# Another order of steps and loads at the start of an attention and FFN kernel

## The chip, the cores and the metric

The kernel runs on one core of a Trainium2 chip. The metric is the time on the device, in microseconds (us), of one execution. The core has five engines with a program each, which run side by side and meet at semaphores: TensorE (PE; its weight loads are shown as PEld), VectorE (DVE), ScalarE (ACT), GpSimdE (POOL) and SyncE (SP), which issues the loads.

## The reference

Eight batches of attention with eight heads, 576 tokens and 64 features to a head; keys and values are means over windows of 8 tokens, so there are 72 of each. Its result is the input of a feed-forward network, 4608 tokens x 512, with 2048 hidden units:

```python
k_p = k.reshape(B, H, Sp, pool, D).mean(axis=3)      # pool = 8, Sp = 72
v_p = v.reshape(B, H, Sp, pool, D).mean(axis=3)
scores = scale * np.matmul(q, k_p.transpose(0, 1, 3, 2))
scores = scores - np.max(scores, axis=-1, keepdims=True)
attn = np.exp(scores)
attn = attn / (np.sum(attn, axis=-1, keepdims=True) + 1e-09)
out = np.matmul(attn, v_p)                           # B x H x S x D
x = out.transpose(0, 2, 1, 3).reshape(B * S, H * D)  # 4608 x 512
h = x @ w_in                                         # 512 x 2048
g = h * (1.0 / (1.0 + np.exp(-1.702 * h)))
y = g @ w_out                                        # 2048 x 512
```

All of it is float32.

## The kernel before

**Tiling.** The work runs in eight rounds. Round b computes the attention of batch b for its 576 tokens; the first 512 go to the FFN as chunk b, and the last 64 of every batch are collected and make a ninth chunk. A batch is handled in two pieces (tokens 0 to 255, and 256 to 575) and, in a piece, in four groups of two heads. FFN products split each float32 operand into a high part that TensorE takes at its fast float32 mode and a low remainder, and add three products (high-high, high-low, low-high). Chunks 0 and 1 go through `dense` (L2217), chunk 0 in two halves of 256 tokens; the other seven through `pair` and `outputs` (L2410, L2621), which save products by sums and differences of quarters.

**Names, which the steps of the prediction use.** `kv`, `tl`: a batch's keys and values, and their last 64 rows, as loaded. `red_k`, `red_v`: sums over windows of 8 tokens; in batch 0 DVE makes the first half of the keys' (`red0_k0`, L1427) and PE the other three by adding eight products with the identity (L1420). `tps`: the windows of the last rows, a product with a 0/1 matrix `members`. `kbd`, `vbd`, `tbd`: these sums laid out block by block with a mask (DVE, L1452 and L1565). `kps` then `k`: the keys transposed by products with the identity `ident`, and copied by ACT (L1632). `qps` then `qt`: the same for q (L1699, copy at L1706). `sps`: scores (L1727). Softmax: `nm` maxima (L1750), `sc` difference (L1758) and exponential on ACT (L1779), sums and reciprocal (L1784 to L1794), `main` and `tail` weights for the first 64 keys of each head and for the last 8 (L1799). `apt`, `tpt`: these transposed (L1871), copied to `ah`, `at`; `pav`: weights by values (L1974, L1977); `x`: its result, split into a high part (ACT, L2008) and a remainder (DVE, L2011). `h`: the first FFN product (L2230 to L2232). `raw`, `e`, `w`: a piece of `w_in` or `w_out` as loaded, its rounding by bits (ACT and DVE shifts, L2136 to L2151) and the cast to the two parts (L2163). `warm`: a product of `ident` with itself whose result nobody uses. In names, `qps0_1_2` is batch 0, piece 1, group 2. A float32 product shows as two records in the trace, or in PE's program as two instructions.

**What sets the order.** The body of the kernel emits nothing; it puts tasks in a list, each with an engine, an estimated duration, what it reads and writes, and a due time. `Plan.order` (L998) simulates the engines with these estimates and returns an order. Two tables written into the file then change it: `PLACES` gives a task's name an offset to its rank in that order, and `SWAPPED` names tasks that run on their other engine: a copy on DVE instead of ACT, or a subtraction, difference or shift on DVE instead of POOL. The offsets carry some 3300 names, and the second table some 510. `WARMS` emits warm-up products right ahead of named tasks:

```python
WARMS = {"PE tps0#0": 16, "PE qps0_0#0": 2, "PE h0_0#0": 2}
order = plan.order()
for n, t in enumerate(order):
    t.rank = n + PLACES.get(t.name, 0)
    if t.name in SWAPPED:
        t.swap()
order.sort(key=lambda t: t.rank)
for t in order:
    for _ in range(WARMS.get(t.name, 0)):
        keep_warm()
    t.emit()
```

Each engine runs its own instructions strictly in that order, and SP issues loads in it too; a ring of buffers (four PSUM banks for `o` and two kinds of two) makes a task wait for an earlier user of its place. So an offset in the table sets which instruction an engine will wait at, and what stands behind it.

Of the kernel before, what the change touches and what calls it, by code (L numbers as in the profile page):

```python
# [19 lines left out]
POOL = 8  # L20
# [20 lines left out]
    "ACT ah0_0#0": 9.64, "ACT ah0_0#1": 9.8235, "ACT ah0_0#2": -10.8, "ACT ah0_0#3": -26.5, "ACT ah0_1#0": 14.6667,  # L41
    "ACT ah0_1#1": 25.0, "ACT ah0_1#3": -14.2857, "ACT ah1_0#0": 66.5, "ACT ah1_0#1": 30.0, "ACT ah1_0#2": 9.8333,
    "ACT ah1_0#3": 28.0769, "ACT ah1_1#0": 63.1852, "ACT ah1_1#1": 59.4444, "ACT ah1_1#2": 81.0,
    "ACT ah1_1#3": 73.6, "ACT ah2_0#0": 97.8462, "ACT ah2_0#1": 15.4545, "ACT ah2_0#2": 56.3077,
    "ACT ah2_0#3": -24.7273, "ACT ah2_1#1": -1.6667, "ACT ah2_1#3": 7.6667, "ACT ah3_0#1": -26.7,
    "ACT ah3_0#2": 50.6667, "ACT ah3_0#3": 38.4444, "ACT ah3_1#0": 13.1818, "ACT ah3_1#1": 16.8571,
    "ACT ah3_1#2": 39.3333, "ACT ah3_1#3": 51.0, "ACT ah4_0#1": -3.3333, "ACT ah4_0#3": 26.125, "ACT ah4_1#2": 3.25,
    "ACT ah5_0#0": -28.3333, "ACT ah5_0#1": -4.5, "ACT ah5_0#2": 5.3333, "ACT ah6_0#0": -86.3333,
    "ACT ah6_0#1": -39.5, "ACT ah6_0#2": -53.5909, "ACT ah6_0#3": -59.5, "ACT ah6_1#1": 4.3333,
    "ACT ah6_1#3": 10.25, "ACT ah7_0#0": -19.0, "ACT ah7_0#3": 7.6667, "ACT ah7_1#0": -19.5, "ACT ah7_1#2": 3.5,  # L50
    "ACT at0_0#1": -28.5, "ACT at0_1#0": -4.0, "ACT at0_1#1": -4.0, "ACT at1_0#0": 77.2667, "ACT at1_0#1": 71.4,
    "ACT at1_1#0": 75.6296, "ACT at1_1#1": 67.1111, "ACT at2_0#0": -4.0, "ACT at2_0#1": 31.7143,
    "ACT at2_1#0": 12.4444, "ACT at3_0#0": 26.0, "ACT at3_0#1": 22.5, "ACT at3_1#1": -4.375, "ACT at4_0#0": -10.5,
    "ACT at4_0#1": -10.4286, "ACT at4_1#1": 4.75, "ACT at5_0#0": -6.5, "ACT at5_0#1": -13.5, "ACT at5_1#1": -2.3333,
    "ACT at6_0#0": -47.6667, "ACT at6_0#1": -48.2857, "ACT at6_1#0": -47.2308, "ACT at6_1#1": -38.0,
    "ACT at7_0#0": -38.25, "ACT at7_0#1": -42.125, "ACT at7_1#0": -43.3333, "ACT at7_1#1": -40.6667,
    "ACT cs2_0#0": 4.75, "ACT cs2_0#2": 2.3333, "ACT cs2_0#5": -5.6, "ACT cs2_0#7": -7.1429, "ACT cs2_1#0": 6.2857,
    "ACT cs2_1#2": 13.6, "ACT cs2_1#4": 11.6667, "ACT cs2_1#5": 3.3333, "ACT cs2_2#0": 8.3333, "ACT cs2_2#3": -6.8,
# [4 lines left out]
    "ACT cs3_0#0": -7.3333, "ACT cs3_0#6": -9.5, "ACT cs3_1#0": 23.2, "ACT cs3_1#1": 14.7143,  # L63
    "ACT cs3_1#2": 27.7143, "ACT cs3_1#6": 11.3333, "ACT cs3_1#7": -3.0, "ACT cs3_2#2": -16.25,
    "ACT cs3_2#5": -3.75, "ACT cs3_2#6": 7.75, "ACT cs3_3#1": -12.7143, "ACT cs3_3#2": 18.2857,
    "ACT cs3_3#3": -13.3333, "ACT cs3_4#0": 13.8333, "ACT cs3_4#2": 23.0, "ACT cs3_4#3": 10.5, "ACT cs3_4#5": 11.8,
    "ACT cs3_4#6": -16.25, "ACT cs3_5#0": 7.4, "ACT cs3_5#1": -4.5, "ACT cs3_5#2": -16.0, "ACT cs3_5#3": -12.8182,
    "ACT cs3_5#4": -21.6667, "ACT cs3_5#6": 17.0, "ACT cs3_6#0": -16.3333, "ACT cs3_6#1": -19.5,
    "ACT cs3_6#2": -1.25, "ACT cs3_6#3": -16.8333, "ACT cs3_6#4": -27.6471, "ACT cs3_6#5": -33.0588,
    "ACT cs3_6#6": -20.1765, "ACT cs3_6#7": -49.75, "ACT cs3_7#0": -38.25, "ACT cs3_7#1": -61.25,  # L70
    "ACT cs3_7#2": -22.6, "ACT cs3_7#3": -57.25, "ACT cs3_7#4": -41.7, "ACT cs3_7#5": -20.0, "ACT cs3_7#7": -2.3333,
    "ACT cs4_0#0": -11.0, "ACT cs4_0#1": -9.0, "ACT cs4_0#4": -5.8, "ACT cs4_0#5": -1.1429, "ACT cs4_0#6": 14.4286,
    "ACT cs4_0#7": 17.2857, "ACT cs4_1#1": 4.5, "ACT cs4_1#5": 8.2, "ACT cs4_1#6": 16.5, "ACT cs4_2#2": -29.0,
# [6 lines left out]
    "ACT cs4_7#6": -50.8571, "ACT cs4_7#7": -3.7143, "ACT cs5_0#2": 17.25, "ACT cs5_0#4": -17.125,  # L80
    "ACT cs5_0#7": -8.5, "ACT cs5_1#0": -6.8333, "ACT cs5_1#1": -8.5, "ACT cs5_1#5": 12.6, "ACT cs5_1#6": 23.5,
# [5 lines left out]
    "ACT cs6_0#5": -6.0, "ACT cs6_0#6": 12.0, "ACT cs6_1#1": -9.75, "ACT cs6_1#3": -4.5, "ACT cs6_1#4": -11.0,  # L87
# [6 lines left out]
    "ACT cs7_0#0": -6.8571, "ACT cs7_0#1": -9.7143, "ACT cs7_0#3": -19.2222, "ACT cs7_0#6": 13.7778,  # L94
    "ACT cs7_1#0": -1.6667, "ACT cs7_1#1": -14.6667, "ACT cs7_1#3": -12.0, "ACT cs7_1#4": -12.4286,
    "ACT cs7_1#5": -14.3333, "ACT cs7_1#7": -4.5, "ACT cs7_2#1": -1.5, "ACT cs7_2#2": 6.0, "ACT cs7_2#7": -3.5,
    "ACT cs7_3#1": 3.0, "ACT cs7_3#5": 3.3333, "ACT cs7_4#0": 8.3333, "ACT cs7_4#1": 3.3333, "ACT cs7_4#5": 3.25,
    "ACT cs7_5#5": 3.25, "ACT cs7_6#5": 3.25, "ACT cs8_0#0": -2.3333, "ACT cs8_0#2": -2.0, "ACT cs8_0#7": -7.6667,
    "ACT cs8_1#0": 7.0, "ACT cs8_2#2": 8.6667, "ACT cs8_2#5": 4.5, "ACT cs8_3#1": 3.0, "ACT cs8_3#5": 3.3333,
    "ACT cs8_4#0": 8.3333, "ACT cs8_4#1": 3.3333, "ACT cs8_4#5": 3.6667, "ACT cs8_5#5": -1.7143,  # L100
    "ACT cs8_6#0": -8.2857, "ACT cs8_6#1": -4.6667, "ACT cs8_6#3": -2.6667, "ACT cs8_6#4": -2.6667,
    "ACT cs8_6#5": -1.3333, "ACT cs8_7#0": -5.5, "ACT cs8_7#1": -3.5, "ACT cs8_7#3": -2.6667,
    "ACT cs8_7#4": -2.6667, "ACT e#10": -89.9, "ACT e#12": 9.0, "ACT e#14": 8.6, "ACT e#15": -5.5,
    "ACT e#16": -5.6667, "ACT e#18": 39.6, "ACT e#20": 29.6667, "ACT e#21": -47.8889, "ACT e#22": 42.7143,
    "ACT e#24": 43.4545, "ACT e#25": 40.7143, "ACT e#26": 30.7273, "ACT e#27": -8.8571, "ACT e#28": 174.5,
    "ACT e#29": 161.1667, "ACT e#3": 42.08, "ACT e#30": 93.5455, "ACT e#31": 173.8, "ACT e#32": 141.6,
    "ACT e#4": -84.6667, "ACT e#5": -6.72, "ACT e#6": -37.0, "ACT e#7": -39.4706, "ACT e#8": -75.8333,
    "ACT e#9": -4.0, "ACT g0_0#2": -55.3333, "ACT g0_0#6": 10.0, "ACT g0_256#1": -51.5, "ACT g0_256#2": -88.2,
    "ACT g0_256#3": -134.8571, "ACT g0_256#5": -32.3077, "ACT g0_256#7": -17.2222, "ACT g1_0#0": 20.0,
    "ACT g1_0#1": 23.5714, "ACT g1_0#11": 14.4545, "ACT g1_0#12": -20.3333, "ACT g1_0#13": -17.1429,  # L110
    "ACT g1_0#15": -24.25, "ACT g1_0#2": -6.6667, "ACT g1_0#4": -15.25, "ACT g1_0#5": -15.6667, "ACT g1_0#6": -8.75,
    "ACT g1_0#7": -27.2857, "ACT gh0_0#0": -7.3333, "ACT gh0_0#2": -52.2, "ACT gh0_0#5": 14.6,
    "ACT gh0_0#6": 10.6667, "ACT gh0_0#7": -9.6667, "ACT gh0_256#1": -55.8, "ACT gh0_256#2": -91.1333,
    "ACT gh0_256#3": -146.7143, "ACT gh0_256#5": -36.0769, "ACT gh0_256#7": -21.6667, "ACT gh1_0#0": 17.0,
    "ACT gh1_0#1": 16.4286, "ACT gh1_0#11": 21.2857, "ACT gh1_0#12": -8.3077, "ACT gh1_0#15": -18.0,
    "ACT gh1_0#2": -7.1111, "ACT gh1_0#4": -25.7778, "ACT gh1_0#5": -6.0, "ACT gh1_0#6": -12.375,
    "ACT gh1_0#8": -4.4286, "ACT gh2_0#0": 6.4, "ACT gh2_1#1": 13.6667, "ACT gh2_1#3": 5.3333, "ACT gh2_2#2": 28.0,
    "ACT gh2_3#0": -18.5, "ACT gh2_3#2": -15.3333, "ACT gh2_3#3": -30.3333, "ACT gh2_4#2": 5.5455,
    "ACT gh2_4#3": -7.6364, "ACT gh2_5#0": 8.8571, "ACT gh2_5#1": 43.5, "ACT gh2_5#3": -12.6667,
    "ACT gh2_6#0": 21.0909, "ACT gh2_6#1": -3.8, "ACT gh2_6#3": -8.2857, "ACT gh2_7#0": 14.4, "ACT gh3_0#2": -7.8,  # L120
    "ACT gh3_1#0": 8.3333, "ACT gh3_1#2": 11.4286, "ACT gh3_2#0": -24.6667, "ACT gh3_2#2": 11.5,
    "ACT gh3_4#0": 22.8, "ACT gh3_4#2": -20.0, "ACT gh3_5#0": -10.6667, "ACT gh3_5#2": 14.3333,
    "ACT gh3_6#1": -30.7647, "ACT gh3_6#2": -16.8824, "ACT gh3_6#3": -45.0, "ACT gh3_7#0": -14.8,
    "ACT gh3_7#1": -29.6, "ACT gh3_7#2": -12.0, "ACT gh4_0#1": 7.5714, "ACT gh4_0#2": 22.1429,
    "ACT gh4_1#1": 9.6667, "ACT gh4_2#0": -22.5, "ACT gh4_2#2": -4.2, "ACT gh4_2#3": -16.75, "ACT gh4_3#1": 30.4,
    "ACT gh4_4#0": 36.3, "ACT gh4_4#1": 15.1667, "ACT gh4_4#2": -5.0, "ACT gh4_4#3": -10.4, "ACT gh4_5#0": 38.75,
    "ACT gh4_5#1": 33.5, "ACT gh4_6#0": 21.7273, "ACT gh4_6#2": -22.3636, "ACT gh4_6#3": -34.8182,
# [2574 lines left out]
```

## Time and profile before

| | |
|---|---|
| three executions | 892.00, 891.79, 890.77 us; median 891.79 |
| the profiled execution | 892.42 us, of which the trace spans 890.6 |
| TensorE clock granted | 1.00 |
| PE busy | 879.3 us (99%) |
| DVE, ACT, POOL busy | 630.1 (71%), 543.8 (61%), 314.6 (35%) |
| start of the trace to the first `h` product | 35.52 us |
| moved by DMA in the span | 176.67 MB, mean 198 GB/s |

The profile is one execution. A row of a timeline has its start, the busy time of a run of like instructions, engine and line, the operation, what it writes and reads, the count, and in brackets how long the engine was idle before it and what it waited for. A row of a list of waits has the total, the number and the longest of such idle times. The time that a group is busy is counted to the end of its last instruction; the next one often starts before that. Line numbers are those of the kernel before; after the change those behind the tables are higher by 11.

### The profile page before, as it was taken

To read this page: it belongs to the slowest core of one execution; us is meant where nothing else is said; L and a number is where in the kernel's file an instruction comes from. 1 tells how busy PE (TensorE), PEld (TensorE's weight loads), DVE (VectorE), ACT (ScalarE), POOL (GpSimd) and SP (SyncE) were. 2 spreads that over 40 slices of the span, in tenths; PEclk is the share of its full clock that TensorE was granted. 3 is DMA by queue.
4 is the path that set the end of the run, shared out by engine and by line. 5 is a ranking of instruction groups with operands and counts; after the bars stand their busy time and mean duration, and the time that the engine had idled before them with its cause. 6 is when DMAs were issued, how large, how long until landed. Compare 5 with 4: busy or idle time off the path is not lost.

```text
span 890.6 us, 15774 instructions
## 1 busy us (share of the span) xinstructions
PE 879.3 (99%) x5432; PEld 785.8 (88%) x5432; DVE 630.1 (71%) x1255; ACT 543.8 (61%) x1245; POOL 314.6 (35%) x309
## 2 busy tenths in 40 slices
PE   7999999999999999999999999999999999999997
PEld 6889988888899998898999998989998989998986
DVE  5877889888888886698878887787677843222332
ACT  4986665356676754667576766686568563344433
POOL 2888565664412233221521161236323460000000
PEclk9999999999999999999999999999999999999999
DMA  9964454657467657678775677667664675556541
GB/s 254 370 223 134 124 151 156 234 200 215 156 202 228 223 181 245 182 226 241 219 218 181 176 233 219 220 203 250 175 205 145 201 235 186 172 190 205 166 142 48
DMA packets 145262, 176.67 MB, mean 198 GB/s; under 512 B 85664, under 2 KB 96928, under 8 KB 145184
## 3 DMA queue, kind: packets, MB, share of 16 engines
q1 hardware_dynamic: 140336, 166.89, 60.5%
q10 hardware_dynamic: 4848, 8.78, 2.8%
q8 instruction: 43, 0.70, 0.3%
q14 instruction: 35, 0.29, 0.1%
HBM read 150.47 MB, written 25.17 MB: 197 GB/s over the span
## 4 chain that ended last, share of the span: by engine, by line
PE 94%; SPq 2%; ACT 1%; DMA 1%; issue 0%; DVE 0%; ACTq 0%
PE ha L2435 18%; PE hb L2435 13%; PE o L2639 12%; PE o L2638 12%; PE o L2637 11%; PE sps L1727 4%; PE h L2230 3%; PE h L2232 3%; PE h L2231 3%; PE o L2274 3%; PE o L2272 3%; PE o L2273 3%; DMA raw<-in_moe_w_out_dram 1%; SPq L1317 1%; PE pav L1966 1%; PE pav L1969 1%
## 5 line engine op out<-in xcount | busy, mean ns | idle before, releaser
L2639 PE MATMUL o<-w,glall 128*128 128x512 f32 x448 | 176.3, 394 | 0.0
L2637 PE MATMUL o<-w,ghall 128*128 128x512 f32 x448 | 176.3, 394 | 0.0
L2638 PE MATMUL o<-w,ghall 128*128 128x512 f32 x448 | 176.0, 393 | 0.0
L2489 POOL TENSOR_TENSOR glall<-shared,ghall 128x256 fp32r<-128x256 f32 x88 | 70.4, 805 | 215.8 <-ACT shared L2482 144.3
L2639 PEld LDWEIGHTS o<-w,glall 128*128 128x128 f32 x448 | 84.2, 188 | 18.5
L2435 PEld LDWEIGHTS ha<-xs,ws 128*128 128x128 f32 x672 | 92.6, 189 | 7.6 <-ACT shared L2450 1.0
L2435 PE MATMUL ha<-xs,ws 128*128 128x256 f32 x672 | 99.2, 283 | 0.0
L2474 ACT ACTIVATE ghall<-shared 128x256 fp32r<-128x256 f32 x150 | 61.5, 415 | 60.9 <-DVE shared L2457 32.5
L2435 PE MATMUL hb<-x,ws 128*128 128x256 f32 x672 | 95.5, 284 | 0.0
L2435 PEld LDWEIGHTS hb<-x,ws 128*128 128x128 f32 x672 | 89.1, 189 | 4.5 <-DVE shared L2457 0.5
L2637 PEld LDWEIGHTS o<-w,ghall 128*128 128x128 f32 x448 | 84.6, 189 | 9.1
L2638 PEld LDWEIGHTS o<-w,ghall 128*128 128x128 f32 x448 | 84.1, 188 | 9.1
L2457 DVE TENSOR_TENSOR shared<-shared,hb 128x256 f32<-128x256 f32 x112 | 46.5, 415 | 55.8 <-PE hb L2435 40.9
L2450 ACT COPY shared<-ha 128x256 f32<-128x256 f32 x94 | 34.8, 370 | 65.0 <-PE ha L2435 63.8
L2489 POOL TENSOR_TENSOR glall<-gall,ghall 128x256 fp32r<-128x256 f32 x45 | 33.4, 746 | 103.4 <-ACT gall L2482 67.9
L2230 PE MATMUL h<-x,w 128*128 128x256 f32 (+1 forms) x192 | 63.0, 328 | 0.7 <-ACT g L2247 0.5
L2482 ACT ACTIVATE shared<-shared 128x256 f32<-128x256 f32 x150 | 61.0, 415 | 3.7 <-ACT osb L2190 0.5
L2232 PE MATMUL h<-x,w 128*128 128x256 f32 (+1 forms) x192 | 61.3, 319 | 0.0
L2231 PE MATMUL h<-x,w 128*128 128x256 f32 (+1 forms) x192 | 61.2, 319 | 0.0
L2260 POOL TENSOR_TENSOR gl<-g,gh 128x512 fp32r<-128x512 f32 x30 | 41.0, 1367 | 50.4 <-ACT gh L2252 35.6
L2489 DVE TENSOR_TENSOR glall<-shared,ghall 128x256 fp32r<-128x256 f32 x62 | 29.5, 477 | 35.8 <-ACT shared L2482 27.3
L2435 PEld LDWEIGHTS ha<-x,shared 128*128 128x128 f32 x336 | 46.7, 189 | 4.8 <-ACT shared L2450 0.8
(193 smaller groups left out, 2039.1 us busy)
## 6 DMA issues: line engine op xcount, KB each, us to landing
ws<-wd SPq DMA_DIRECT2D x168, 512.0 KB
shared<-wd SPq DMA_DIRECT2D x56, 256.0 KB
out_dram<-osb ACTq DMA_DIRECT2D x32, 256.0 KB
wd<-stage SPq DMA_DIRECT2D x16, 512.0 KB
raw<-in_moe_w_in_dram SPq DMA_DIRECT2D x15, 512.0 KB
raw<-in_moe_w_out_dram SPq DMA_DIRECT2D x15, 512.0 KB
kv_False<-in_k_dram SPq DMA_DIRECT2D x28, 256.0 KB
kv_True<-in_v_dram SPq DMA_DIRECT2D x28, 256.0 KB
```

Source lines behind the costliest of these rows:

```text
L2230: nc.tensor.matmul(o, lhsT=w[:, 0, j], rhs=xs[:, 0], start=j == 0, stop=False)
L2231: nc.tensor.matmul(o, lhsT=w[:, 1, j], rhs=xs[:, 0], start=False, stop=False)
L2232: nc.tensor.matmul(o, lhsT=w[:, 0, j], rhs=xs[:, 1], start=False, stop=j == NJ - 1)
L2260: engine.tensor_tensor(out=gl(), in0=g(), in1=gh().bitcast(F32), op=ALU.subtract)
L2435: nc.tensor.matmul(o, lhsT=wv()[:, r, jj], rhs=xo(k, jj), start=start and n == 0, stop=n == len(terms) - 1,  skip_group_check=not start,)
L2457: lambda: nc.vector.tensor_tensor(out=part(i), in0=part(i), in1=hb()[:, half * 256 : half * 256 + 256], op=ALU.add),
L2474: lambda: nc.scalar.activation(out=gh(), in_=src(), func=AF.Gelu_apprx_sigmoid),
L2482: lambda: nc.scalar.activation(out=part(i), in_=src(), func=AF.Gelu_apprx_sigmoid),
L2489: engine.tensor_tensor(out=gl(), in0=part(i), in1=gh().bitcast(F32), op=ALU.subtract)
L2637: nc.tensor.matmul(o(), lhsT=gh()[:, tok], rhs=w()[:, 0], start=start, stop=False)
L2638: nc.tensor.matmul(o(), lhsT=gh()[:, tok], rhs=w()[:, 1], start=False, stop=False)
L2639: nc.tensor.matmul(o(), lhsT=gl()[:, tok], rhs=w()[:, 0], start=False, stop=stop)
```

## The change

The change lies in the two tables alone: 1139 of the offsets in `PLACES` differ, and in `SWAPPED` 36 names are gone and 40 are new. No function, no estimate and not `WARMS` is touched, and the arithmetic is as it was. From about the middle of chunk 1 the programs of PE, and further on those of the other engines, are the same again: the last 4305 of PE's 5203 instructions stand in the same order, the last 1015 of DVE's, 1075 of ACT's, 217 of POOL's and 473 of SP's. PE's instructions are the same in number, and so are SP's; DVE has six more.

Two rows or so of the tables, as an example:

```diff
@@ PLACES @@
-    "DMA kv0#3": 8.1, "DMA kv0#4": -5.5, "DMA kv0#5": -4.3333, "DMA kv0#6": -32.3, "DMA kv0#7": -38.4,
+    "DMA kv0#0": 3.3, "DMA kv0#4": 52.75, "DMA kv0#5": 46.625, "DMA kv0#6": 15.2, "DMA kv0#7": 23.8889,
...
+    "PE qps0_0#0": -16.7143, "PE qps0_0#1": -18.5714, "PE qps0_1#0": -37.4, "PE qps0_1#1": -41.25,
...
@@ SWAPPED @@
+    "ACT main7_1#8", "ACT qt0_0#0", "ACT qt0_0#1", "ACT qt0_0#2", "ACT qt0_1#2", "ACT qt0_1#3", "ACT stage#11",
 WARMS = {"PE tps0#0": 16, "PE qps0_0#0": 2, "PE h0_0#0": 2}
```

What that makes of the engines' programs is seen in their first rows. A row is a line of the kernel, the operation, what it writes and reads with buffer numbers, the size, and a count where alike instructions follow each other.

SP, the first loads. Before:

```order
L2105 DMA raw4_131<-in_moe_w_in_dram 128x4x256
L1317 DMA kv0_145<-in_k_dram 128x1x512 x2
L1378 DMA tl0_148<-in_k_dram 64x8x64
L1378 DMA tl0_148<-in_v_dram 64x8x64
L2539 DMA q0_0_151<-in_q_dram 128x8x64 x2
L2105 DMA raw0_154<-in_moe_w_in_dram 128x4x256
L1317 DMA kv0_156<-in_k_dram 128x1x512 x2
```

Now:

```order
L2550 DMA q0_0_131<-in_q_dram 128x8x64 x2
L1389 DMA tl0_147<-in_v_dram 64x8x64
L1389 DMA tl0_147<-in_k_dram 64x8x64
L2116 DMA raw0_174<-in_moe_w_in_dram 128x4x256
L1328 DMA kv0_181<-in_k_dram 128x1x512 x2
L2116 DMA raw4_189<-in_moe_w_in_dram 128x4x256
L1328 DMA kv0_198<-in_k_dram 128x1x512 x2
```

The q tiles come first, and the first keys behind the last rows and a weight piece.

PE, the start of the program. Before:

```order
L2600 MATMUL warm_135<-ident_79 128x128 x17
L1556 MATMUL tps0_188<-tl0_148,members_141 128x512
L2600 MATMUL warm_135<-ident_79 128x128 x2
L1699 MATMUL qps0_0_0_196<-ident_79,q0_0_151 128x128 x2
L1699 MATMUL qps0_0_1_199<-ident_79,q0_0_151 128x128 x2
L1607 MATMUL kps0_0_202<-ident_79,kbd0_190 128x64x2 x2
```

Now:

```order
L2611 MATMUL warm_136<-ident_79 128x128 x2
L1710 MATMUL qps0_0_0_139<-ident_79,q0_0_131 128x128 x2
L1710 MATMUL qps0_0_1_142<-ident_79,q0_0_131 128x128 x2
L2611 MATMUL warm_136<-ident_79 128x128 x16
L1567 MATMUL tps0_170<-tl0_147,members_150 128x512
L1618 MATMUL kps0_0_200<-ident_79,kbd0_193 128x64x2 x2
```

The q transposes have moved ahead of `tps0`; of the warm-up products, which go with their tasks, 16 now stand between the two.

DVE, after its masks are made, up to the first keys. Before:

```order
L1427 TENSOR_REDUCE red0_k0_159<-kv0_145 128x128
L1452 TENSOR_TENSOR kbd0_190<-red0_k0_159,mask2i_84 128x256
L1565 TENSOR_TENSOR tbd0_192<-tps0_188,mask_90 128x512
L2151 TENSOR_SCALAR raw4_131<-e4_133 128x512
L1750 TENSOR_REDUCE nm0_0_220<-sps0_0_0_215 128x2x2
```

Now:

```order
L1576 TENSOR_TENSOR tbd0_172<-tps0_170,mask_90 128x512
L2162 TENSOR_SCALAR raw0_174<-e0_176 128x512
L1717 COPY qt0_0_0_187<-qps0_0_0_139 128x256
L1438 TENSOR_REDUCE red0_k0_191<-kv0_181 128x128
L1463 TENSOR_TENSOR kbd0_193<-red0_k0_191,mask2i_84 128x256
```

The layout of the last rows, a weight piece's shift and a q copy that ACT made before stand ahead of the first key sum.

PE again, from the last scores of piece 0 of batch 0. Before:

```order
L1727 MATMUL sps0_0_3_279<-k20_211,qt0_0_3_270 128x144 x2
L1420 MATMUL red0_v1_287<-kv0_165,ident_79 128x128 x8
L1699 MATMUL qps0_1_0_309<-ident_79,q0_1_168 128x128 x2
L1699 MATMUL qps0_1_0_309<-ident_79,q0_2_170 128x64
L1699 MATMUL qps0_1_1_313<-ident_79,q0_1_168 128x128 x2
L1699 MATMUL qps0_1_1_313<-ident_79,q0_2_170 128x64
L1420 MATMUL red0_v0_326<-kv0_222,ident_79 128x128 x8
L1871 MATMUL apt0_0_3_360<-ident_79,main0_0_353 128x128 x2
L1871 MATMUL apt0_0_2_363<-ident_79,main0_0_353 128x128 x2
L1871 MATMUL tpt0_0_372<-ident_79,tail0_0_358 64x128 x2
```

Now:

```order
L1738 MATMUL sps0_0_2_266<-k20_217,qt0_0_2_256 128x144 x2
L1710 MATMUL qps0_1_1_285<-ident_79,q0_1_245 128x128 x2
L1710 MATMUL qps0_1_1_285<-ident_79,q0_2_283 128x64
L1710 MATMUL qps0_1_0_290<-ident_79,q0_1_245 128x128 x2
L1710 MATMUL qps0_1_0_290<-ident_79,q0_2_283 128x64
L1882 MATMUL tpt0_0_306<-ident_79,tail0_0_304 64x128 x2
L1431 MATMUL red0_v1_316<-kv0_294,ident_79 128x128 x8
L1882 MATMUL apt0_0_3_325<-ident_79,main0_0_310 128x128 x2
L1882 MATMUL apt0_0_0_333<-ident_79,main0_0_310 128x128 x2
```

The transposes of the softmax's tail (`tpt0_0`) now stand ahead of both value sums.

1387 rows, old and new, of tables (PLACES, SWAPPED) are left out of this document.

## The prediction

> **What bounds the kernel now.** I read the table of stretches first, because one share over 890 us says nothing of the stage that the change touches. Its columns are the stretch, its length, the busy time of PE, PEld, DVE, ACT and POOL with instruction counts, the granted clock, the DMA share and GB/s.
>
> ```profile
> 0.00:36.00 36.00, 30.43 (x193) 26.23 (x193) 22.23 (x51) 22.42 (x46) 15.36 (x19) 1.00 0.96 293
> 36.00:260.00 224.00, 223.10 (x1278) 193.73 (x1277) 191.86 (x329) 142.85 (x277) 136.42 (x115) 1.00 0.58 183
> 260.00:850.00 590.00, 589.81 (x3752) 534.57 (x3751) 403.87 (x847) 363.69 (x889) 162.80 (x176) 1.00 0.66 206
> ```
>
> From 36 us on PE is busy without a gap, and PE's instructions are the same in number before and after. So the change can be paid only where PE stands: 5.6 us of the first 36, and the last fraction of a microsecond behind. Next the list of PE's waits, first up to 36 us, then (last two rows) behind it; columns are total, count and longest.
>
> ```profile
> PE sps L1727 <- ACT k L1632: 1.2, 2, 0.7
> PE red_k L1420 <- DMA kv<-in_k_dram: 1.1, 1, 1.1
> PE tps L1556 <- DMA tl<-in_v_dram: 0.9, 1, 0.9
> PE qps L1699 <- DVE sps L1784: 0.5, 1, 0.5
> PE kps L1607 <- DVE kbd L1452: 0.3, 1, 0.3
> PE kps L1613 <- DVE tbd L1565: 0.2, 1, 0.2
> ...
> PE h L2230 <- ACT g L2247: 0.5, 1, 0.5
> ...
> PE h L2230 <- ACT x L2008: 0.2, 1, 0.2
> ```
>
> Third, PE's timeline, for when each step of the first batch runs (start, busy time of the group, what, and idle before it):
>
> ```profile
> 8.65 1.10 PE L1556 MATMUL tps<-tl,members 128*128 128x512 f32 x2 [0.92 <-DMA tl<-in_v_dram]
> ...
> 10.56 0.43 PE L1607 MATMUL kps<-ident,kbd 128*128 128x128 f32 x2
> ...
> 14.83 2.02 PE L1420 MATMUL red_k<-kv,ident 128*128 128x128 f32 x16 [1.08 <-DMA kv<-in_k_dram]
> 16.69 0.38 PE L1699 MATMUL qps<-ident,q 128*128 128x128 f32 x2
> 17.37 0.44 PE L1607 MATMUL kps<-ident,kbd 128*128 128x128 f32 x2 [0.30 <-DVE kbd L1452]
> 17.64 0.53 PE L1613 MATMUL kps<-ident,tbd 128*128 128x32 f32 x4
> 18.83 1.25 PE L1727 MATMUL sps<-k,qt 128*128 128x144 f32 x8 [0.66 <-ACT k L1632]
> 19.99 2.02 PE L1420 MATMUL red_v<-kv,ident 128*128 128x128 f32 x16
> ...
> 25.67 0.63 PE L1871 MATMUL apt<-ident,main 128*128 128x128 f32 x4
> ...
> 32.47 1.99 PE L1727 MATMUL sps<-k,qt 128*128 128x144 f32 x12
> ...
> 35.52 0.36 PE L2230 MATMUL h<-x,w 128*128 128x256 f32 x1
> ```
>
> Nearly everything is a chain here: key sums, keys, scores, softmax, first FFN product `h` at 35.52. Whatever delays `h` is paid in full, since nothing idles behind it that could take it back, beyond the last two waits of the list, .7 us.
>
> **The change, part by part.** *Loads, then the warm-up.* The q tiles are loaded first now, and their four transposes (`qps0_0_0`, `qps0_0_1`) stand on PE ahead of `tps0`. But the 16 warm-up products are tied to `tps0`, so they stand between the two. Before, the same products ran while the loads were awaited. Their price, in two halves of that stretch:
>
> ```profile
> 1.36:6.21 4.85, 4.85 (x22) 4.85 (x23) 1.00 0.89 257
> 6.35:7.57 1.22, 1.22 (x13) 1.20 (x11) 1.00 0.99 200
> ```
>
> So .22 us a record until PE has worked 4.85 us, and .094 after it, though the granted clock reads 1.00 in both. When q lands I take from the first load:
>
> ```profile
> 4.42 0.63 ACT L2136 ACTIVATE e<-raw 128x512 f32<-128x512 f32 x1 [2.40 <-DMA raw<-in_moe_w_in_dram]
> ...
> 8.12 1.91 DVE L1427 TENSOR_REDUCE red_k<-kv 128x128 f32<-128x1024 f32 x1 [4.78 <-DMA kv<-in_k_dram]
> 10.07 0.42 DVE L1452 TENSOR_TENSOR kbd<-red_k,mask2i 128x256 f32<-128x256 f32 x1
> 10.41 0.68 DVE L1565 TENSOR_TENSOR tbd<-tps,mask 128x512 f32<-128x512 f32 x1
> 11.01 0.68 DVE L2151 TENSOR_SCALAR raw<-e 128x512 uint32<-128x512 uint32 x1
> ...
> 0.73 0.46 SPq L2105 DMA_DIRECT2D raw<-in_moe_w_in_dram  x1
> 1.25 1.32 SPq L1317 DMA_DIRECT2D kv<-in_k_dram  x2
> ```
>
> 512 KB issued at .73 were used at 4.42, 3.7 us later; two issues of 256 KB take 1.32, so the second q tile is issued at 1.4 and the pair lands between 4.4 and 6.9 (the key load took 8.12 - 1.25 = 6.9 from issue, competing with others); the q tiles compete with nothing, and I take 5.1. Four cold transposes, about .3 each as the first ones out of idle: 6.3. Of 32 warm records, those until 5.1 + 4.85 = 9.95 are slow, (9.95 - 6.3)/.22 = 17, and 15 at .094 follow: `tps0` starts at 11.4. Bounds: q at 4.4 and all fast, 8.6 to 8.9; all slow, 13.3. Before: 8.65.
>
> *VectorE's order.* DVE now has `tbd0` (needs `tps0`), a weight piece's shift and a q copy ahead of the key sum `red0_k0`, which before was done at 10.0, not waiting for PE at all. So the key sum now waits for PE, and PE for the key sum. `tps0` ends 11.4 + 1.1 = 12.5; `tbd` .60 (10.41 to 11.01), shift .60, copy .40 (as `kbd`, of 256 columns), sum 1.95 (8.12 to 10.07), `kbd` .42: `kps0_0` starts at 16.5, against 10.56: **+6.0**. PE idles 4 us for it.
>
> *Scores.* From there the products stand without loads to wait for. Back to back: two times `kps` .7 (17.37 to 18.17 less the drain), key sum of the second half 1.86 (14.83 to 16.69), two scores .58 each (18.83 to 19.99), four q transposes .44 give 21.4. The copies go at ACT's prices:
>
> ```profile
> 17.82 0.64 ACT L2136 ACTIVATE e<-raw 128x512 f32<-128x512 f32 x1
> 18.38 0.40 ACT L1632 ACTIVATE k<-kps 128x288 f32<-128x288 f32 x1
> 18.67 0.37 ACT L1706 COPY qt<-qps 128x256 f32<-128x256 f32 x1
> ...
> 21.34 0.68 ACT L1779 ACTIVATE sc<-sc 128x576 f32<-128x576 f32 x1 [0.59 <-DVE sc L1758]
> ```
>
> `kps0_1` ends at 21.0; key copy .40, the piece `e2` .58, q copy .37: the last two scores run at 22.4, end 23.5. Before they ended, with `red_v` behind, at 19.99: **+3.5**; of the 6.0, 2.5 came back as the waits for loads and copies of before (1.08, .30, .66, .50) have mostly gone.
>
> *Softmax.* Before, behind the scores stood one value sum (`red_v`), six q transposes and the second value sum, until the transposes of the weights at 25.67: 5.7 us, in which PE's only wait was .48. Now `tpt0_0`, which needs the tail of the softmax, stands six q transposes (1.1 us) behind the scores and both value sums stand behind it.
>
> ```profile
> 19.63 0.95 DVE L1750 TENSOR_REDUCE nm<-sps 128x4 f32<-128x288 f32 x2 [1.35 <-PE sps L1727]
> 20.49 0.81 DVE L1758 TENSOR_TENSOR sc<-sps,nm 128x288 f32<-128x288 f32 x2
> ...
> 22.81 0.75 DVE L1784 TENSOR_REDUCE sps<-sc 128x8 f32<-128x576 f32 x1
> ...
> 24.11 1.42 DVE L1799 TENSOR_TENSOR main<-sc,sps 128x256 f32<-128x256 f32 x4
> ```
>
> The first of the two scores is there at 23.0. From it: maxima and differences 1.6 (19.63 to 21.22 as the next group began), exp .69, sum and reciprocal 1.30 (22.81 to 24.11), tail .28, semaphores between engines, some .8: 27.7. PE idles from 24.6 to 27.7, **3.1 us**, which before the value sums covered.
>
> *To the end of the stage.* Before, from 19.99 to 35.52 less .48, PE worked 15.05. Of that 1.1 (the six transposes) is done; three score products (`sps0_1_2`, six records of 1.99/12, .91 with the piece that follows) have moved behind the first `h`; .2 of warm-up comes in. So `h` starts at 27.7 + 13.26 = 41.0, and the same work stands at 41.9: **+6.3**.
>
> *Given back.* Behind `h` PE stood .9 us to 260 (224.00 - 223.10) and .2 to 850 (590.00 - 589.81). A chain that comes late finds some of what it waited for there; between nothing and 1.1 I take 1.0, since both rows of the list behind 36 us wait for engines that are given 5 us more: **+5.3** net. The other swaps (36 copies or subtractions changed engine one way, 40 the other; DVE's instructions are up by six) lie on engines that are 86%, 64% and 61% busy in 36 to 260 us beside a full PE; I cost them at nothing, and at .4 us a copy where one would stand on the path.
>
> Sum: profiled run 892.42 + 5.3 = 897.7; that run lay .63 above the median 891.79, so **897.1 us**.
>
> **Rivals.** *The clock falls back.* The rows show PE slow for its first 4.85 us of work and fast after. If the 4 us of standing at 12.5 make it slow again, the next 22 records' worth of work costs 4.85 instead of 22 x .094 = 2.1; a stage that is partly waiting pays 2 to 2.8 of that: about 899.5. For it: no stop of before after 8 us was longer than 1.08, so the rows can't exclude it. Against: nor do they show one. The Trainium skill ("TensorE: Matmul & The Clock Gate", Part 1: The HAM clock gate) says that one idle window of about 3.4 us throttles PE again to half its clock and that the windows run freely; the slow start agrees with it (22 records in 4.85 us), the falling back no run here shows. By that rule a 4 us stop holds a whole window in one case of six (.6 of 3.4), and a 3.1 us stop in none.
>
> *SP stands in the way.* Later a q piece of batch 1 is ahead of weight pieces in SP's queue and waits for DVE's copy `qt1_0_1`.
>
> ```profile
> SPq L1399 <- DVE qt L1711: 12.0, 2, 8.1
> ```
>
> Before, SP stood 8.1 us in such a place and PE lost nothing; now it would be some 14 us, from 46 to 60. If the weights have 6 us less lead than that, PE pays part of it: +1 to +4, 898 to 901.
>
> *The other side: the front is a wait for loads, and the delay is swallowed.* The six waits of the list before 36 us are 4.2 us, and a chain that starts late finds all loads there. With warm records at .094 `tps0` starts at 8.9 and `kps0_0` at 14.0, +3.5; if the softmax then keeps up, so that `tpt0_0` waits less than .3, all 3.5 comes back: 891.6 to 892.2. Were the warm-up free as well (finished before q is in), `kps0_0` would be at 11.3, and 889 would come out. It decides at two points: `tps0` by 8.9 and no wait ahead of `tpt0_0`. Against: the 32 records stand behind the q transposes, 3.0 us at the fast price; and 1.1 us of cover for a softmax that took 25.5 - 19.6 = 5.9 with other work in it, and 4.7 by the sum above.
>
> **How the numbers follow.** The chain as summed .58; the clock falls back .20; SP in the way .10; the delay is swallowed .12, of which .07 ends within .2% (1.8 us, about what this measurement tells from none) and .05 below. So slower .88, same .07, faster .05. Low end: `tps0` at 8.9 takes 2.5 off 5.3, and a softmax without the .8 for semaphores takes .7: 893.9. High end: all warm records slow +1.9 and one slow stretch +2.5: 897.1 + 4.4 = 901.5. Range 893.9 to 901.5.
>
> **What would show it.** Right: `tps0` at 10.5 to 12; a PE wait of about 4 us before `kps0_0` with DVE's `kbd` as releaser, none of it on a load; a wait of 2 to 4 us before `tpt0_0`; first `h` at 40 to 42; from 60 us on, PE's order shifted by a constant 5 us with no wait over 1 us. Wrong: `kps0_0` before 13, `tpt0_0` without a wait, or an `h` before 37; or `h` on time and a new PE wait between 60 and 170 us on weights.

## The result, and the profile after

The changed kernel takes **901.33 us** (median of four executions, 900.63 to 902.56), the kernel before in the same session 891.28: a ratio of 1.0114, 95% interval 1.0096 to 1.0131, so 10.0 us slower. The forecast was slower, 897.1 us in a range of 893.9 to 901.5: the sign is right, the loss about double. The profiled execution took 902.56 us, its span 900.8; the one of before 892.42 and 890.6.

The same table of stretches as before the change, now of the changed kernel:

```profile
0.00:36.00 36.00, 23.81 (x121) 20.77 (x122) 17.71 (x42) 13.04 (x24) 9.62 (x14) 0.81 0.99 318
36.00:260.00 224.00, 223.12 (x1277) 193.46 (x1276) 185.75 (x326) 148.32 (x284) 126.83 (x110) 1.00 0.56 173
260.00:850.00 590.00, 589.82 (x3764) 535.03 (x3763) 409.65 (x861) 366.17 (x894) 163.12 (x177) 1.00 0.67 205
```

PE's busy time behind 36 us is the same to .02 us. In the first 36 us it falls from 30.43 to 23.81, and a figure that read 1.00 before now reads 0.81: the granted clock. PE's waits up to 45 us, and then its timeline at the places that the prediction named:

```profile
PE kps L1618 <- DVE kbd L1463: 4.0, 1, 4.0
PE tpt L1882 <- DVE tail L1810: 2.8, 1, 2.8
...
PE sps L1738 <- ACT qt L1717: 0.8, 1, 0.8
PE qps L1710 <- DVE sc L1769: 0.7, 1, 0.7
```

```profile
5.41 4.96 PE L2611 MATMUL warm<-ident 128*128 128x128 f32 x32
10.20 1.02 PE L1567 MATMUL tps<-tl,members 128*128 128x512 f32 x2
15.25 0.69 PE L1618 MATMUL kps<-ident,kbd 128*128 128x128 f32 x2 [4.02 <-DVE kbd L1463]
...
16.45 3.76 PE L1431 MATMUL red_k<-kv,ident 128*128 128x128 f32 x16
...
24.92 0.58 PE L1710 MATMUL qps<-ident,q 128*128 128x128 f32 x3
...
29.66 0.61 PE L1882 MATMUL tpt<-ident,tail 128*64 128x128 f32 x2 [2.83 <-DVE tail L1810]
30.06 3.62 PE L1431 MATMUL red_v<-kv,ident 128*128 128x128 f32 x16
...
45.52 0.36 PE L2241 MATMUL h<-x,w 128*128 128x256 f32 x1
```

Both stops are where and as long as forecast. What was not in the sum is the row behind each of them: the same 16 records of a window sum that took 2.02 us before take 3.76 and 3.62. The first FFN product starts at 45.52 instead of 35.52. From there to the end of the span it is 855.3 us, against 855.1 before (900.8 - 45.52, 890.6 - 35.52): **the whole loss is made before the first `h`**, and nothing behind it adds to it.

The table of stretches cut where the granted clock changes shows what slowed the sums (the clock is the third figure from the end):

```profile
11.37:14.79 3.42, 0.00 (x0) 0.00 (x0) 3.38 (x5) 1.02 (x2) 1.33 (x2) 1.00 1.09 363
14.79:21.61 6.82, 6.36 (x29) 6.36 (x30) 1.83 (x4) 2.29 (x5) 2.05 (x2) 0.50 1.04 285
21.61:28.44 6.83, 3.66 (x27) 2.84 (x25) 5.90 (x13) 4.49 (x10) 2.73 (x3) 1.00 1.02 363
28.44:35.27 6.83, 5.14 (x22) 4.33 (x22) 3.30 (x10) 2.23 (x6) 2.08 (x3) 0.50 1.08 391
```

PE ran at half clock from 14.79 to 21.61, behind the first stop, and from 28.44 to 35.27, behind the second.

### The profile page after: what moved, and what is told of

It reads as the page before. It is cut to its first block, busy times and chain, and to the rows that moved or that the text cites. A ratio compares the mean times of both kernels' runs of the same rounds, so it can differ in the third digit from the quotient of the medians.

```text
span 900.8 us, 15770 instructions
## 1 busy us (share of the span) xinstructions
PE 882.8 (98%) x5432; PEld 789.6 (88%) x5432; DVE 627.5 (70%) x1261; ACT 546.5 (61%) x1248; POOL 299.6 (33%) x300
## 4 chain that ended last, share of the span: by engine, by line
PE 91%; DVE 3%; DMA 2%; SPq 1%; issue 1%; ACT 1%; POOL 0%; DVEq 0%; POOLq 0%
PE ha L2446 18%; PE hb L2446 13%; PE o L2650 11%; PE o L2649 11%; PE o L2648 11%; PE sps L1738 4%; PE h L2243 2%; PE h L2241 2%; PE h L2242 2%; PE o L2283 2%; PE o L2284 2%; PE o L2285 2%; PE pav L1977 1%; PE pav L1980 1%; PE pav L1979 1%
## 5 line engine op out<-in xcount | busy, mean ns | idle before, releaser
L2446 PE MATMUL ha<-x,ws 128*128 128x256 f32 x336 | 50.1, 285 | 0.0
```

Source lines behind the costliest of these rows:

```text
L2446: nc.tensor.matmul(o, lhsT=wv()[:, r, jj], rhs=xo(k, jj), start=start and n == 0, stop=n == len(terms) - 1,  skip_group_check=not start,)
```

## The experiments

Two theories stood after this. **Order and clock**: the stops cost what was forecast, and each throttles PE besides. **Loads**: the sums are slow, or the stops long, for loads that contend or come late. The experiments move single tasks in the finished order with a helper, or change `WARMS`; no arithmetic changes in any of them.

```diff
+    def put(what, ahead_of):
+        t = next(t for t in order if t.name == what)
+        order.remove(t)
+        order.insert(next(i for i, o in enumerate(order) if o.name == ahead_of), t)
```

**1. Both stops filled with warm-up products.**

```diff
-WARMS = {"PE tps0#0": 16, "PE qps0_0#0": 2, "PE h0_0#0": 2}
+WARMS = {"PE tps0#0": 16, "PE qps0_0#0": 2, "PE h0_0#0": 2, "PE kps0_0#0": 16, "PE tpt0_0#0": 10}
```

> The changed kernel with warm-up products put into PE's two long stops: 16 (32 records) ahead of the first kps0_0, 10 ahead of tpt0_0. Nothing that is computed changes. Theory 'clock' (the stops themselves cost what was forecast, and each also throttles PE, so that the key sum behind the first took 3.76 us instead of 2.02 and the value sum behind the second 3.62): granted clock 1.00 from 12 us on, key sum and value sum near 2.0, h some 4 us earlier, 896.5 to 898 us. Theory 'loads' (PE is slow behind the stops since its operands or PSUM are contended by loads at 370 to 430 GB/s): both sums stay at 3.6 to 3.8, 901 us or more. The stop ahead of kps0_0 then shows as warm records, and kps0_0 starts at 15 to 15.5 under both.

898.38 us, ratio 1.0076 (1.0056 to 1.0096), granted clock .999 to 1. Useless work took 2.95 us off the median, and 4.1 off the profiled execution (898.43 against 902.56). PE's timeline of this kernel:

```profile
16.16 0.44 PE L1618 MATMUL kps<-ident,kbd 128*128 128x128 f32 x2 [0.52 <-DVE kbd L1463]
...
16.80 2.03 PE L1431 MATMUL red_k<-kv,ident 128*128 128x128 f32 x16
...
22.80 0.58 PE L1710 MATMUL qps<-ident,q 128*128 128x128 f32 x3
...
27.54 0.38 PE L1882 MATMUL tpt<-ident,tail 128*64 128x128 f32 x2 [0.40 <-DVE tail L1810]
27.75 1.95 PE L1431 MATMUL red_v<-kv,ident 128*128 128x128 f32 x16
...
41.23 0.36 PE L2241 MATMUL h<-x,w 128*128 128x256 f32 x1
```

`kps0_0` starts no earlier, but both sums are back at 2.0 and `h` is 4.3 us earlier. The loads are as before, so it isn't they that slowed the sums: it is the clock. This kernel is also the changed order without the clock's part, and it lands on the forecast's own chain: 16.16 (16.5 there), 27.54 (27.7), 41.23 (41.0). Part of that closeness is luck: in this execution the clock first rose at 9.91 us, by chance where the sum had it (9.95), and in that of the changed kernel at 7.96. So `kps0_0` started .9 us later here, and from `kps0_0` to `h` the two differ by 5.2 us (25.1 against 30.3).

**2. A third of that filling**: 6 and 4 products instead of 16 and 10.

> The changed kernel with a third of the filling: 6 warm-up products (1.3 us) ahead of the first kps0_0 and 4 (.9 us) ahead of tpt0_0. It tells what makes PE fall to half clock. In the traces so far the granted clock changed only at ends of windows of 3.413 us, and fell at the end of windows in which PE was busy for none, 26, 30, 32, 38 and 42% of the time, and held through windows of about 70%. Theory 'half-empty window': with so little work in the stops, windows of 30 to 45% remain, and the clock falls in most runs at one place at least: 899 to 901 us, granted clock .995 to .998. Theory 'whole empty window' (only a window without any work throttles): it never falls, granted clock .999 or 1, time as with the full filling, 897.5 to 898.8 us.

900.71 us, but the four executions spread from 896.88 (granted clock 1.0) over 899.98 (.997) and 901.43 (.998) to 904.37 (.991). The profiled one is the last. Its stretches, cut in the same way:

```profile
8.49:11.90 3.41, 3.41 (x27) 2.93 (x27) 0.38 (x1) 1.07 (x2) 0.00 (x0) 1.00 0.97 332
11.90:15.31 3.41, 0.92 (x9) 0.73 (x7) 3.38 (x5) 1.29 (x3) 1.59 (x2) 1.00 1.09 369
15.31:22.14 6.83, 6.63 (x30) 6.64 (x31) 1.81 (x5) 2.02 (x4) 1.78 (x2) 0.50 1.03 291
22.14:25.55 3.41, 2.56 (x22) 2.23 (x20) 2.71 (x7) 2.37 (x5) 0.22 (x1) 1.00 0.98 345
25.55:28.97 3.42, 2.05 (x14) 1.44 (x12) 3.13 (x6) 2.27 (x5) 2.66 (x3) 1.00 1.06 377
28.97:39.21 10.24, 8.40 (x36) 7.59 (x37) 4.24 (x13) 4.41 (x9) 5.36 (x5) 0.50 1.07 349
```

PE worked .92 of 3.41 us (27%) ahead of the first fall and 2.05 (60%) ahead of the second. So a window need not be empty. The spread of 7.5 us in one kernel goes with the clock at its two ends. Where the windows lie against the kernel's start differs from one execution to the next: in the traces of the changed order and its variants, the clock first rose anywhere from 7.92 to 11.35 us. That this phase makes the spread is inferred, since only the slowest of the four has a trace.

**3. The key sum first on DVE**, as before the change: `tbd0`, the shift of weight piece 0 (with the work that follows from it) and the copy `qt0_0_0` behind it.

```diff
+    put("DVE tbd0#0", "PE kps0_0#0")
+    put("DVE raw#0", "PE kps0_0#0")
...
+    put("ACT qt0_0#0", "PE kps0_0#0")
```

> The changed kernel, where DVE makes the key sum red0_k0 and its layout kbd0 ahead of tbd0, of the shift of weight piece 0 and of the q copy qt0_0_0, as before the change; all else as changed. Theory 'order' (PE stood 4.0 us only because DVE put work that waits for tps0 ahead of a key sum whose load had landed by 9.2 us): the stop falls to below 1 us, kps0_0 at 11.7 to 12.2, PE is not throttled there, h 5 to 6.5 us earlier: 895 to 896.5 us. Rival 'loads' (the key load is as late as the stop): kps0_0 at 14 or later, 900 us or more.

898.18 us, ratio 1.0078 (1.0062 to 1.0095): 3.2 us less, where 5 to 6.5 were expected. PE's timeline:

```profile
12.56 0.44 PE L1618 MATMUL kps<-ident,kbd 128*128 128x128 f32 x2
...
13.96 2.05 PE L1431 MATMUL red_k<-kv,ident 128*128 128x128 f32 x16
...
25.11 0.61 PE L1882 MATMUL tpt<-ident,tail 128*64 128x128 f32 x2 [2.82 <-DVE tail L1810]
25.51 3.62 PE L1431 MATMUL red_v<-kv,ident 128*128 128x128 f32 x16
...
40.97 0.36 PE L2241 MATMUL h<-x,w 128*128 128x256 f32 x1
```

The first stop and its half clock are gone, `h` is 4.6 us earlier here; the second stop and its half clock stand unchanged, later in the same chain. That the first stop was DVE's order and no late load is shown. `kps0_0` came at 12.56, not by 12.2 as expected: in this execution the second q tile was used at 5.44 instead of 4.72 and the clock first rose at 9.99 instead of 7.96.

**4. The value sum ahead of `tpt0_0` on PE**, as before the change.

```diff
+    put("DMA kv0#7", "PE tpt0_0#0")
+    put("PE red0_v1#0", "PE tpt0_0#0")
```

> The changed kernel, where PE's value sum red0_v1 stands ahead of tpt0_0 again; all else as changed. Theory 'order and clock': the value sum (1.9 us) covers most of the 2.8 us stop, the half-idle stretch that throttled PE the second time is gone, and the value sum takes 2.0 instead of 3.6: 3 to 4 us less, 897.3 to 898.3 us. Rival 'loads' (the values have not landed, so the sum would only stand there itself): within 1 us of the changed kernel. Theory 'order alone' (no throttling): 1.9 less, 899.4 us.

903.08 us, ratio 1.0132 (1.0114 to 1.015): nothing gained, all theories missed. Its waits on PE tell why, with ACT's rows and the one of PE that waits for them:

```profile
PE kps L1618 <- DVE kbd L1463: 4.0, 1, 4.0
...
PE apt L1882 <- ACT qt L1717: 1.6, 1, 1.6
...
PE tpt L1882 <- DVE tail L1810: 0.8, 1, 0.8
```

```profile
30.72 0.36 ACT L1912 COPY at<-tpt 32x256 f32<-32x256 f32 x1 [0.97 <-PE tpt L1882]
31.10 0.65 ACT L2156 ACTIVATE raw<-raw 128x512 uint32<-128x512 uint32 x1
31.78 0.42 ACT L1717 COPY qt<-qps 128x320 f32<-128x320 f32 x1
...
32.26 0.69 PE L1882 MATMUL apt<-ident,main 128*128 128x128 f32 x2 [1.58 <-ACT qt L1717]
```

The stop before `tpt0_0` falls from 2.8 to .8, and a new one of 1.6 appears right behind it: `apt0_0_3` waits for a place in PSUM that ACT's copy `qt0_1_1` must empty, and on ACT that copy stands behind the copy of the tail that `tpt0_0` makes. The wait had been there, hidden under the value sum. And the stretch stays half empty (42% busy in the window ahead of it), so PE fell to half clock a little later. The move was not worth nothing, though: from `kps0_0` to `h` the profiled execution takes 29.1 us (17.29 to 46.39), the changed kernel's 30.3. But it started `kps0_0` 2.0 us later, with the second q tile used at 5.52 instead of 4.72 and the clock first risen at 11.35 instead of 7.96.

**5. Both moves together.**

> The changed kernel with both moves (DVE's key sum first, PE's value sum ahead of tpt0_0). If these two places carry the whole loss, as by the ledger of the traces, the sum of the two gains, 8.5 to 10 us, comes back: 891.5 to 893 us, within .2% of the kernel before. If other parts of the change (swaps, later loads) cost or gain something too, it ends elsewhere: above 894 if they cost, below 890 if they gain.

898.3 us, ratio 1.0078 (1.0057 to 1.01), no better than the first move alone; `apt0_0_3` waits 1.59 us as in experiment 4. Two places do not carry the whole loss.

**6. A third move**: `qt0_1_1` ahead of `qt0_1_0` on ACT.

```diff
+    put("ACT qt0_1#1", "ACT qt0_1#0")
```

> The changed kernel with the key sum first on DVE, the value sum ahead of tpt0_0 on PE, and a third move: ACT copies qt0_1_1 ahead of qt0_1_0, so ahead of the copy of the softmax's tail (at0_1). With the first two moves alone PE stood 1.6 us before the first apt, for the place in PSUM that qt0_1_1 frees and that stood on ACT behind at0_1. Theory 'order' (the waits of batch 0 hang together, and each is where an engine's queue has the wrong thing in front): that stop goes, the half-empty stretch with it, so PE keeps its clock: h at 36.5 to 38 instead of 39.9, 893.5 to 895.5 us. Rival 'softmax bounds it' (the chain of DVE and ACT from the last score to the weights is as long as it is): the stop only moves to the next product that needs the weights, h at 39 or later, 896.5 us or more.

896.1 us (894.54 to 897.39), ratio 1.0064 (1.0047 to 1.0081). In the profiled execution (894.54, clock 1.0) the stop of 1.6 has become one of .6 for the softmax's weights and `h` starts at 37.59, inside what "order" expected; the median lies .6 us above its range. The other three ran at .996 to .999 and took 1.4 to 2.9 us longer. They have no trace, so it is inferred and not shown that with stops of .4 to .9 us close together this order keeps the clock only by luck of the phase.

**7. Fewer warm-up products ahead of `tps0`** (6 for 16), with both stops filled, and **8.** the same with the three moves.

> The changed kernel with both long stops filled, as in the run above of that kind, but with 6 instead of 16 warm-up products ahead of tps0. If the warm-up between the q transposes and tps0 lies on the path, as the prediction had it, tps0 starts 1.5 to 2.2 us earlier (fewer records, though more of them at half clock) and all behind it: 896 to 897 us, against 898.4 with 16. If tps0 waits for something else (its load, the 0/1 matrix), no change.

> The changed kernel with the three moves (key sum first on DVE, value sum ahead of tpt0_0 on PE, copy qt0_1_1 ahead on ACT) and 6 instead of 16 warm-up products ahead of tps0. With the three moves kps0_0 started at 12.6, with tps0 at 10.8; the key sum's layout was ready .7 us behind tps0. If the warm-up is on the path there too, but only until the key load (landed by 9.2) takes over: kps0_0 at 11.7 to 12, and with fewer records to warm up, sums at half clock somewhat longer: .3 to 1 us less than 896.1 us, so 895.1 to 895.8. If the longer half clock eats it: 896 or more.

With filled stops 896.34 us, ratio 1.0062 (1.0047 to 1.0077), 2.0 less than experiment 1, or 1.4 with each set against the kernel before of its own session: `tps0` starts at 8.15 instead of 11.05, and `h` at 39.21 instead of 41.23. The warm-up between the q transposes and `tps0` was on the path. With the three moves 896.92, nothing gained: `kps0_0` starts at 12.20 instead of 12.58, because the key sum takes over as the bound (PE waits 2.10 us for `kbd`, .75 before), and the two runs at .993 and .994 took 3 us longer than those at .998.

**9. One part of the change alone on the kernel before: DVE's order** (`tbd0` and a shift ahead of the key sum), and **10. the order of the first loads.**

> The kernel before with one part of the change alone: DVE makes tbd0 and the shift of its first weight piece ahead of the key sum red0_k0 and its layout. Theory 'order': kps0_0 moves from 10.6 to 13.3; the waits for the next key load (1.08) and for copies swallow half of it: h 1.2 to 1.8 us later, 892.5 to 893.2 us with the clock kept; where the 2.6 us stop falls so into a window of the clock gate that it throttles PE, 1.5 to 3 more, 894 to 896 us. Rival 'swallowed' (a front bound by loads): within .5 us of before, 891 to 891.7.

> The kernel before with one other part of the change alone: its first loads in the order of the changed kernel (both q tiles, last rows, weight piece 0, the first keys, piece 2, the second keys), every engine's own order as before. By the landings of the changed kernel (first keys at 9.2 us instead of 8.0, second at 12.4 instead of 14.7, piece 2 at 11.2 instead of 4.4) kps0_0 starts 1 to 1.2 us later, the wait for the second keys (1.08) goes, and ACT stands for piece 2 ahead of the first q copy, some 1.3 us. Theory 'the loss is in the engines' order, not in the loads': the value sums start within .5 us of before and the whole is 890.5 to 891.8 us. Rival 'the loads carry part of the loss': 892.5 to 895 us.

894.40 against 890.62 us, ratio 1.0041 (1.0026 to 1.0056), and 894.47 against 891.63, ratio 1.0036 (1.0022 to 1.005). The rows on PE and DVE, first with DVE's order, then with the loads:

```profile
13.37 0.44 PE L1607 MATMUL kps<-ident,kbd 128*128 128x128 f32 x2 [2.63 <-DVE kbd L1452]
...
37.48 0.36 PE L2230 MATMUL h<-x,w 128*128 128x256 f32 x1
```

```profile
12.58 0.44 PE L1607 MATMUL kps<-ident,kbd 128*128 128x128 f32 x2 [3.18 <-DVE kbd L1452]
...
17.25 3.15 PE L1420 MATMUL red_k<-kv,ident 128*128 128x128 f32 x16
...
38.55 0.36 PE L2230 MATMUL h<-x,w 128*128 128x256 f32 x1
...
10.19 1.88 DVE L1427 TENSOR_REDUCE red_k<-kv 128x128 f32<-128x1024 f32 x1 [6.85 <-DMA kv<-in_k_dram]
```

Either part makes a stop ahead of `kps0_0`, and in both profiled executions (clock .997 and .996) PE is throttled behind it. With the loads I expected no loss; the first keys were used at 10.19 instead of 8.12, so the stop of 3.2 us is the load's here. In the changed kernel it isn't seen: there DVE reached the key sum at 12.80, when the keys had landed (experiment 3 uses them at 10.12).

**11 and 12. A better order of loads for the kernel before?** Keys, last rows and q first, then two weight pieces, then values, with the roundings of the later pieces moved down on ACT, DVE and POOL, and with 8 warm-up products more on PE; the second run also puts three copies on ACT ahead of them.

> The kernel before with its first loads in an order of need: all keys, last rows and q tiles first, then weight pieces 2 and 0, the values and the rest of q, and pieces 1 and 3 behind them; the copies and shifts that wait for the pieces moved down on ACT, DVE and POOL accordingly, and 8 warm-up products put ahead of the third score and of the value sum to keep the clock. In the kernel before, PE waited .92 and 1.08 us for loads and its value sums began as the values landed. If the loads bound the front there, kps0_0 starts at 9 instead of 10.6, the value sum at 18 instead of 20, h 1.5 to 3 us earlier: 888.5 to 890 us. If the softmax or the decoding of weights takes the place of the loads, 891 or more; if PE, with the same work and more gaps, loses its clock, 892 to 895.

> The kernel before with its first loads in order of need, as in the run above of that kind, but with ACT's copies ah0_0_2, ah0_0_0 and qt0_1_3 ahead of the roundings of weight pieces whose loads come late. In that run batch 0 was 2 us ahead of the kernel before until 24.6 us, then PE stood 2.4 us for an ACT copy behind roundings that waited for loads, and lost its clock. If that queue on ACT was the only cause: no stop over 1 us, h at 33 to 34.5 against 35.5, 888.5 to 890 us, faster than before. If the decoding of weights is now too late for the first products, a wait of h on a cast w appears and 891 or more comes out.

896.02 us, ratio 1.0057 (1.0042 to 1.0072), and 897.31, ratio 1.0063 (1.0049 to 1.0076): both slower than before. PE's longest waits, first run and second:

```profile
PE apt L1871 <- ACT ah L1949: 2.4, 1, 2.4
PE sps L1727 <- ACT k L1632: 1.6, 2, 1.1
```

```profile
PE sps L1727 <- ACT k L1632: 2.0, 2, 1.5
PE pav L1974 <- DVE x L2011: 1.8, 1, 1.8
PE sps L1727 <- ACT ah L1949: 1.5, 1, 1.5
```

`kps0_0` came at 8.7 instead of 10.6 in both. In the first run the first transposes of the weights were still 2.0 us ahead (23.70 against 25.67); then PE stood at copies queued behind the roundings of weights, which had become late, and `h` came at 38.16. Putting three copies ahead turned that stop into several others, the longest of 1.8 and 1.5 us, and `h` came at 39.62. No kernel of this study beats the one before.

## Why the prediction was right in sign and short by half

*Loads and warm-up.* Right: the 32 records stand on the path (experiment 7). `tps0` came at 10.20, not 11.4, because the q tiles were in by 4.72, not 5.1, and PE was throttled for less long after they came: until 7.96, 3.2 us of work, where the sum took the 4.85 of the row of before.

*VectorE's order.* Right: a stop of 4.02 us released by `kbd`, 4 forecast; taken away by DVE's order alone (experiment 3).

*Scores.* Forecast end 23.5; PE went on at 24.92 in the changed kernel and at 22.80 with its clock kept. The term is right but for the clock.

*Softmax.* The stop of 2.83 us is there, 3.1 forecast; one of .71 ahead of it was not seen. From the first of the last two scores to `tpt0_0` it took 5.2 us (24.4 to 29.66), .5 more than the sum's 4.7, in which the .8 for semaphores has no row of its own. What the sum did not see either is that "which the value sums covered before" holds only while ACT empties PSUM in time: putting the sum back gave nothing (experiment 4), until a copy on ACT moved too (experiment 6).

*Given back.* .7 instead of 1.0: from `h` to the end it is .2 longer than before, with .9 us of scores moved behind `h`.

*SP in the way*: SP stood longer than forecast, 22.6 us instead of some 14, and still no PE wait behind 45 us is over .4. Right to cost it at nothing here.

**The step that failed is the rival "the clock falls back".** It had a chance of .20, one stop, and 2.4 us, and was kept out of the likeliest sum. It came at both stops and cost 4.3 us in the profiled executions (45.52 against 41.23) and 2.95 in the medians. Its price for one stop was near (2.4, against 4.3 for two); its chance and the number of stops were too low. The sum with it, 897.7 + 4.3 = 902.0, would have met the profiled 902.56. The chance was too low because I asked whether a whole empty window fits into a stop ("one case of six", "in none"). The rule that I weighed (the Trainium skill, "TensorE: Matmul & The Clock Gate", Part 1: The HAM clock gate) has the clock throttled after one idle window of about 3.4 us. On the window the runs agree: in every trace the granted clock changed only at whole multiples of 3.41 us from its first change. On "idle" they go further. The window ahead of the first fall was empty, which the rule asks for and the phase made so; the one ahead of the second, 25.03 to 28.44, was 32% busy (1.09 us), and the clock fell all the same. So a row of short waits counts as a stop.

The order's own part is 6.0 us by the profiled executions (898.43 against 892.42), where 5.3 was forecast, and 7.2 by the medians of experiment 1 (898.38 against 891.22); the two differ because the profiled execution of the kernel before was 1.2 us slower than that median. The filling itself doesn't lengthen the stops, since PE still waits .5 and .4 us at its ends. So of the 4.2 us between 897.1 and 901.33 the clock explains 2.95; the other 1.3 remain where the clock is kept, and which term is short by them stays open. In experiment 6, with three places put back, the profiled `h` still starts 2.1 us later than before, and the median is still 5.5 us above that of the kernel before (896.1 against 890.62), clock included; which of the other moved tasks carry that wasn't taken apart.

## What to carry to other kernels

Where TensorE is the bound, a wait that makes it stand for 2 us or more is to be priced twice: the stop, and the work behind it at half clock for one to three windows of 3.4 us. Each of the nine stops of 2.1 to 4.0 us in these traces was followed by it. So filling a stop with work nobody uses can pay at once, and an order is better judged by the busy share of TensorE in each 3.4 us than by its longest wait. When an instruction is moved back to where it stood, its neighbours on other engines have to come along: the same place in PSUM, an engine's queue behind it and a load behind that turned each repair here into the next wait.

## What the runs showed of the hardware

The windows were the surprise. Over the first 45 us of the fourteen profiled executions, PE's busy share in the 3.41 us ahead of each possible change sorts the outcomes almost cleanly:

| PE's clock in the window | then | busy share of the window |
|---|---|---|
| full | fell to half, 13 times | 0 to .48, once .60 |
| full | stayed | .55 and more, once .47 |
| half | rose to full | .85 and more |
| half | stayed | up to .86, once .94 |

So about half a window of work holds the clock, and nearly a whole one is needed to get it back; between .47 and .60 the rows contradict each other, which may be matmul ends that are modelled. And the column of the granted clock read 1.00 in the first microseconds of every execution, while the warm-up records took .22 us each: it shows a fall, but not that PE began at half clock.
